# Longer DMA times in a planner, wider chunk spacing, split key buffers and one constant tile for two scans

## Chip, cores and metric

One NeuronCore of a Trainium2 chip runs the whole program in one launch. The metric is the device time of one execution in microseconds, and several executions are given by their median. The engines are named as in the profile: PE is TensorE, DVE is VectorE, ACT is ScalarE, POOL is GpSimd, and SP is the queue engine that issues nearly all DMAs of this kernel.

## What is computed

The reference has three stages, all in float32: a gated linear attention over 4 batches, 8 heads, 768 steps and 48 features, then two feed-forward stages over the 3072 tokens that come out of it.

```python
for t in range(S):                       # attention, S = 768
    state = alpha[:, :, t, :, None] * state + einsum('bhd,bhe->bhde', k[:, :, t], v[:, :, t])
    y[:, :, t] = einsum('bhd,bhde->bhe', q[:, :, t], state)
x = y.transpose(0, 2, 1, 3).reshape(3072, 384)
x = ((x @ w_a) * (x @ w_b)) @ w_out      # first feed-forward stage, 384 -> 1536 -> 384
h = x @ w_in                             # second, 384 -> 2048 -> 384
out = (maximum(h, 0) + alpha * minimum(h, 0)) @ w_out2
```

## The kernel before

**Tiling.** The tokens are cut into 6 blocks of 512 columns (`MB`). A block is made of four chunks of 128 steps, one for each batch, so there are 24 chunks, g = 4n + c for block n and batch c. The feed-forward matmuls run on pairs: each float32 operand is split into a high and a low part, and one product costs three passes (lines 926, 927 and 929). A *step* of the first stage is two up projections (tiles `pa` and `pb`, nine matmuls of 128x512 each) and, two steps later, the down projection (`acc`, nine matmuls); there are 12 steps a block. Blocks 0 and 1 are interleaved in halves, and blocks 2 to 5 follow whole. The second stage comes after all of the first, on results kept in DRAM.

**A chunk.** Its inputs come by three loads: `ra` (the decays, line 561), `kq` (keys and queries, line 565) and `v` (line 569). DVE runs a scan backwards (`scan_r`, line 584), a reciprocal of four columns (`recip`, line 590), a scan forwards (`scan_a`, line 594), and the product of both with keys and queries (`mul`, line 599). The first scan has a constant tile `ones` as its additive operand (zeros, and a one at the head of each of the four rows), the second a tile `invs` of the same form whose heads are the reciprocals. PE then computes scores, and two bursts follow: `pe_cross` (lines 786 and 808) and `pe_own` (lines 786 and 793, and from block 2 on also the scores of the next chunk, line 625). The last burst therefore waits for the next chunk's `mul` as well. Between the two bursts DVE updates the state (line 813, `As`).

From block 2 on (`BY_BLOCKS`) the keys are needed turned. DVE transposes them in 32x32 squares (`turn`, line 660), four DMAs store them in DRAM (`away`, line 664, `ktd<-kt`), and four bring them back (`back`, line 674, `ks<-ktd`). The tiles `kt` and `ks` share one buffer: line 678 lets the turn wait, through the ring `kring`, for the burst that used the keys of the chunk before.

**Buffers.** `ra`, `kq` and `v` have two buffers each. A `Ring` (line 281) hands over the operations that the next user of a buffer waits for. A `kq` load waits for all users of the chunk two earlier, its `pe_own` among them. The x tile of block n takes the buffer of block n-2 (line 1071).

**The order.** It is no written list. Each operation is handed to a planner, `Graph`, by `add` (line 81), with its engine, a planned duration, a key, and for a DMA a latency on top. `place` (line 112) lays the operations out in planned time: each engine takes the ready one with the lowest key. `latest` (line 199) goes back from the end and gives each its latest start as a new key. `search` (line 231) then moves keys of operations that begin before `SOON` = 120 us at random, 1500 times, and keeps what ends sooner on PE, also with durations and latencies drawn a little larger (`SEED`, `TRIES`, `WORLDS`, line 55). The program is emitted in the order found, and each engine executes its part strictly in that order. Where the plan has a pause of PE of over 0.5 us before the start of block 2, dummy matmuls are put in for 70% of it (`fill`, line 339, tile `wp`; they read `ones` without its first column).

**Keys and planned times that the change touches.** A chunk of block n from 2 on gets the key `block_at[n] - (BC - c) * 12000 - 14000` (line 535, in nanoseconds; `block_at` is the planned start of the block). Planned for its DMAs are, as duration plus latency in ns: `ra` 720 + 3000, `kq` 1400 + 3000, `v` 720 + 3000 (lines 577 to 579), each store of turned keys 430 + 2000 (line 680), each return 350 + 3800 (line 684). Between engines 250 ns (`HOP`) are added.

Of the kernel before, what the change touches and what calls it, by code (L numbers as in the profile page):

```python
# [14 lines left out]
F32 = mybir.dt.float32  # L15
BF16 = mybir.dt.bfloat16
# [4 lines left out]
ALU = mybir.AluOpType  # L21
# [4 lines left out]
P = 128  # L26
CH = 128
HC = CH // 2
BC = 4
MB = BC * CH  # L30
SQ = 32
BT = P // SQ
# [5 lines left out]
LAG = 2  # L38
SPLIT = ((0, 0), (1, 0))
BY_BLOCKS = 2  # L40

ON_PE = (("a", 0), ("b", 0), ("o", 0))

# [8 lines left out]
SLACK = 500  # L52
SWITCH = 100
SOON = 120000
SEED, TRIES, WORLDS = 2, 1500, 2


class Op:
# [10 lines left out]
class Graph:  # L69
# [11 lines left out]
    def add(self, eng, dur, fn, key, deps=(), lat=0, after=(), pool=None, burst=False, line=None):  # L81
        o = Op()
        o.pool, o.hold, o.burst = pool, [], burst
        o.eng, o.dur, o.fn, o.key, o.lat = eng, dur - LEAD.get(eng, 0), fn, key, lat + LEAD.get(eng, 0)
        o.users, o.soft, o.n = [], [], len(self.ops)
        for d in {x.n: x for x in deps if x is not None}.values():
            d.users.append(o)
        for d in {x.n: x for x in after if x is not None}.values():
            d.soft.append(o)
        if line:  # L90
            if line in self.last and self.last[line] not in [x for x in after if x is not None]:
                self.last[line].soft.append(o)
            self.last[line] = o
        self.ops.append(o)
        return o
# [203 lines left out]
def body(tc, akq, v, vg, w_a, w_b, w_o1, w_in, w_o2, beta, out):  # L299
    nc = tc.nc  # L300
# [5 lines left out]
    NJ = H // 2  # L306
    D = KT * P // H
    GR = 64 - D
    NA = NJ * (CH + 1) + 1
    NC = NJ * CH  # L310
    NB = NG // BC

    with ExitStack() as ctx:
        ctx.enter_context(tc.manual_schedule())
        pool = lambda name, bufs=1, **k: ctx.enter_context(tc.tile_pool(name=name, bufs=bufs, **k))
        const, wpool, pers = pool("const"), pool("wpool"), pool("pers")
        xpool, cpool, gpool, tp = pool("xpool", 2), pool("cpool", 2), pool("gpool", 2), pool("tp", 2)
# [7 lines left out]
        ident = plus.bitcast(F32)  # L325
        mask = const.tile([P, P], F32, name="mask")
        betaT = const.tile([P, F2], F32, name="betaT")
        ones = pers.tile([P, NJ, CH + 1], F32, name="ones")
        invs = pers.tile([P, NJ, CH + 1], F32, name="invs")
        Z = pers.tile([P, BC, NJ, D], F32, name="Z")  # L330
        At = pers.tile([P, 2 * NC], F32, name="As")
        x2d = [dram.tile([P, 2, KT, MB], F32, name=f"x2d{n}") for n in range(NB)]
        w2d = [dram.tile([P, 2 * UC], F32, name=f"w2d{i}") for i in range(2 * NU2)]
        ktd = [dram.tile([SQ, NJ, BT, P], F32, name=f"ktd{g}") for g in range(NG)]


        warm = ones.bitcast(BF16)[:, 0, 2 : 2 + 2 * CH]

        def fill(t0, t1):
            wp = ps_mm.tile([P, MB // 2], F32, name="wp", tag="mm")  # L340
            for _ in range(int((t1 - t0) * 0.7) // 110):
                nc.tensor.matmul(wp, warm[:, 0:P], warm, start=True, stop=True)

        nc.gpsimd.memset(ones, 0.0)
        nc.gpsimd.memset(ones[:, :, 0:1], 1.0)
        nc.gpsimd.memset(invs, 0.0)
        make_identity(nc, eye)
        nc.gpsimd.memset(mask, 1.0)
        nc.gpsimd.affine_select(
            out=mask, in_=mask, pattern=[[1, P]], compare_op=ALU.is_ge, fill=0.0,  # L350
# [18 lines left out]
        due, block_at = {}, {}  # L369
# [131 lines left out]
        for u in range(NU1):  # L501
            for nm, src in (("a", w_a), ("b", w_b), ("o", w_o1)):
                x = nm, u
# [16 lines left out]
        st = [dict() for _ in range(NG)]  # L520
        xt, xuse, xdone, xpart = {}, {}, {n: [] for n in range(NB)}, {}
        xring, lring, rring, vring = Ring(2), Ring(2), Ring(2), Ring(2)
        aring, kring, sring = Ring(1), Ring(1), Ring(1)
        both = ps_att.tile([P, 2, 2 * NC // 2], F32, name="both")
        yfree, afree = [], []
        att = lambda nm: ps_att.tile([P, NJ, CH], F32, name=nm, tag="att")
        before = {"scan": None}
        accfree = [[] for _ in range(KT)]
        state = [[] for _ in range(BC)]
        sums = [At[:, NC + i * NJ * D : NC + (i + 1) * NJ * D].rearrange("p (j d) -> p j d", d=D) for i in range(2)]  # L530
        slots = [Z[:, c] for c in range(BC)] + sums[1:]

        def place(g):
            n, c = divmod(g, BC)
            key = c * 1000 - 100000 if n == 0 else block_at[n] - (BC - c) * 12000 - 14000
            if n == 1:
                key = block_at[n] - (BC - c) * 9500 - 6000

            def A(eng, dur, fn, deps, early=0, lat=0, after=(), line=None):
                return G.add(eng, dur, fn, key - early, deps, lat, after, burst=eng == "PE", line=line)  # L540

            return st[g], n, c, n == 0, A

        def inputs(g):
            s, n, c, start, A = place(g)
# [28 lines left out]
            kT = lambda: s["kq"][:, 0]  # L574
            qT = lambda: s["kq"][:, 1]
            r0 = lambda: s["ra"][:, 0 : NA - 1].rearrange("p (j t) -> p j t", j=NJ)[:, :, 0:1]
            la = A("SP", 1000 if g == 0 else 720, load_a, rwait, 14000, 2400 if g == 0 else 3000, line="ra")
# [5 lines left out]
            def scan_r():  # L583
                nc.vector.tensor_tensor_scan(
                    out=s["ra"][:, 0 : NA - 1][:, ::-1], data0=s["ra"][:, : NA - 1 : -1],
                    data1=ones.rearrange("p j t -> p (j t)"), initial=0.0, op0=ALU.mult, op1=ALU.add,
                )

            def recip():
                nc.vector.reciprocal(invs[:, :, 0:1], r0())  # L590

            def scan_a():
                a = s["ra"][:, NA - 1 : 2 * NA - 2]
                nc.vector.tensor_tensor_scan(out=a, data0=a, data1=invs.rearrange("p j t -> p (j t)"),
                                             initial=0.0, op0=ALU.mult, op1=ALU.add)

            def mul():
# [1 line left out]
                nc.vector.tensor_tensor(out=s["kq"], in0=s["kq"], in1=f[:, :, :, 1:], op=ALU.mult)  # L599

            turned = n >= BY_BLOCKS
            r = A("DVE", 1220, scan_r, [la])
            rc = A("DVE", 180, recip, [r, before["scan"]])
            sa = before["scan"] = A("DVE", 1220, scan_a, [rc])
            slack = SLACK if not start else 0
            k1 = q1 = A("DVE", 1220, mul, [lq, sa], 0, slack)
            rhold.append(k1)
# [33 lines left out]
        def chunk(g):  # L641
            s, n, c, start, A = place(g)
# [3 lines left out]
            kT, qT, r0, r, k1, lv = (s[x] for x in ("kT", "qT", "r0", "r", "k1", "lv"))  # L646
# [9 lines left out]
                slots[c], slots[BC] = new, old  # L656

            def turn():
                s["kt"] = tp.tile([P, NJ, P], F32, name="kt", tag="ks", bufs=1)
                nc.vector.transpose(s["kt"], kT())  # L660

            def away(b):
                def f():
                    nc.sync.dma_start(
                        ktd[g].rearrange("t j a f -> t (j a) f")[:, :, b * SQ : (b + 1) * SQ],
                        s["kt"][b * SQ : (b + 1) * SQ].rearrange("p j (a d) -> p (j a) d", d=SQ),
                    )
                return f

            def back(a):  # L670
                def f():
                    if a == 0:
                        s["ks"] = tp.tile([P, NJ, P], F32, name="ks", tag="ks", bufs=1)
                    nc.sync.dma_start(s["ks"][a * SQ : (a + 1) * SQ], ktd[g][:, :, a, :])
                return f

            if turned:
                x = A("DVE", 650, turn, [k1, *kring.take()])
                lhold.append(x)
                moved = [A("SP", 430, away(b), [x], 0, 2000) for b in range(BT)]  # L680
                x = None
                back_at = []
                for a in range(BT):
                    x = A("SP", 350, back(a), moved, 0, 3800, after=[x])
                    back_at.append(x)

            zs = None
# [16 lines left out]
            if start:  # L704
# [3 lines left out]
                x = A("PE", 560, s["keys"], [k1, *w0])  # L708
                pa = A("PE", 1120, s["scores"], [k1, *w1, *w2])
            elif "front" in s:  # L710
                x = pa = s["front"]
# [5 lines left out]
            if turned:  # L717
                ks = back_at
# [531 lines left out]
```

## Time and profile before

| | us |
|---|---|
| median of 3 runs | 942.45 |
| lowest and highest | 941.32, 942.47 |
| the profiled execution | 943.25 |
| its span, first to last instruction | 941.50 |

| engine | busy us | share |
|---|---|---|
| PE | 932.5 | 99% |
| PE weight load | 760.1 | 81% |
| DVE | 564.0 | 60% |
| ACT | 245.2 | 26% |
| POOL | 2.2 | 0% |

The profile is of one execution, and its times count from the first instruction. Busy time doesn't tell useful from dummy matmuls; these have the tile `wp`. In the rows below a timeline gives start, duration, engine, line, operation and tiles (written <- read), and in brackets how long the engine had been idle before and who released it. "kq<-in_akq" is a load, "SPq" the issuing of DMAs on SP. The granted clock of PE is full in all stretches.

### The profile page before, as it was taken

The page shows a single profiled execution, that of the slowest core. Times are in us where ns is not written, and L with a number is a line of the kernel's source. Part 1 is how long each engine was busy: PE and PEld are TensorE (multiplying, and loading weights), DVE is VectorE, ACT ScalarE, POOL GpSimd, SP SyncE. Part 2 cuts the span into 40 slices and gives each one's busy share as a digit, 9 for nine tenths or more (in the row PEclk, how much of TensorE's full clock was granted, in tenths as well). Part 3 has the DMA queues.
Part 4 walks back from the last instruction along what each step waited for, and adds up shares of the span by engine and source line. Part 5 has one row for each costly group of instructions (what it writes and reads, how often), then busy time and mean ns, then how long its engine had stood idle before and what let it go on. Part 6 is the DMA issues. An engine that isn't in the chain of part 4 may idle for free.

```text
span 941.5 us, 15646 instructions
## 1 busy us (share of the span) xinstructions
PE 932.5 (99%) x6637; PEld 760.1 (81%) x6637; DVE 564.0 (60%) x865; ACT 245.2 (26%) x406; POOL 2.2 (0%) x11
## 2 busy tenths in 40 slices
PE   9999999999999999999999999999999999999998
PEld 7788887888888788787888888888888888888886
DVE  8999964674886687663232264554545545545554
ACT  3555531223333333331122121111111111111111
POOL 0000000000000000000000000000000000000000
PEclk9999999999999999999999999999999999999999
DMA  9973103563657767763266620100200200200000
GB/s 353 403 262 102 32 1 79 159 189 137 210 162 228 249 207 217 241 175 93 82 235 202 212 91 1 68 34 1 89 12 1 101 1 0 101 1 1 34 0 34
DMA packets 75238, 112.89 MB, mean 120 GB/s; under 512 B 38689, under 2 KB 48417, under 8 KB 75169
## 3 DMA queue, kind: packets, MB, share of 16 engines
q1 hardware_dynamic: 75024, 111.77, 36.1%
q8 instruction: 52, 0.85, 0.4%
q14 instruction: 18, 0.14, 0.0%
q10 hardware_dynamic: 144, 0.13, 0.0%
HBM read 78.97 MB, written 30.93 MB: 117 GB/s over the span
## 4 chain that ended last, share of the span: by engine, by line
PE 90%; DVE 5%; DMA 2%; issue 1%; SPq 1%; ACT 0%; DVEq 0%; ACTq 0%
PE acc L926 12%; PE acc L929 12%; PE acc L927 12%; PE pi L926 7%; PE pi L927 7%; PE pi L929 7%; PE pb L926 5%; PE pa L926 5%; PE pb L927 5%; PE pa L929 5%; PE pa L927 5%; PE pb L929 5%; PE both L786 2%; PE both L625 1%; DMA v<-in_v 1%; DMA ra<-in_akq 1%
## 5 line engine op out<-in xcount | busy, mean ns | idle before, releaser
L950 ACT CAST gh<-ng 128x512 fp32r<-128x512 f32 x96 | 59.5, 620 | 329.8 <-DVE ng L1163 274.0
L1159 DVE TENSOR_SCALAR ng<-pi,betaT 128x512 f32<-128x512 f32 x96 | 72.1, 751 | 105.6 <-PE pi L929 104.7
L954 DVE TENSOR_TENSOR gl<-ng,gh 128x512 fp32r<-128x512 f32 x96 | 66.3, 690 | 79.6 <-ACT gh L950 79.6
L926 PE MATMUL pi<-x,v 128*128 128x512 f32 x288 | 113.3, 393 | 0.0
L929 PE MATMUL acc<-gl,v 128*128 128x512 f32 x288 | 113.1, 393 | 0.0
L926 PE MATMUL acc<-gh,v 128*128 128x512 f32 x288 | 112.9, 392 | 0.0
L927 PE MATMUL pi<-x,v 128*128 128x512 f32 x288 | 112.7, 391 | 0.0
L927 PE MATMUL acc<-gh,v 128*128 128x512 f32 x288 | 112.1, 389 | 0.0
L1057 DVE TENSOR_TENSOR a_sb<-a_sb,pb 128x512 f32<-128x512 f32 (+1 forms) x76 | 49.9, 656 | 83.3 <-PE pb L929 83.3
L926 PE MATMUL pb<-x,wb 128*128 128x512 f32 (+1 forms) x228 | 87.8, 388 | 0.6 <-DVE a_sb L1057 0.6
L926 PE MATMUL acc<-gh,wo 128*128 128x512 f32 (+1 forms) x228 | 88.4, 388 | 0.0
L926 PE MATMUL pa<-x,wa 128*128 128x512 f32 (+1 forms) x228 | 87.3, 386 | 0.0
L929 PE MATMUL acc<-gl,wo 128*128 128x512 f32 (+1 forms) x228 | 86.8, 381 | 0.0
L927 PE MATMUL pb<-x,wb 128*128 128x512 f32 (+1 forms) x228 | 86.0, 380 | 0.5 <-DVE wb L453 0.5
L927 PE MATMUL acc<-gh,wo 128*128 128x512 f32 (+1 forms) x228 | 86.4, 379 | 0.0
L927 PE MATMUL pa<-x,wa 128*128 128x512 f32 (+1 forms) x228 | 85.9, 380 | 0.0
L950 ACT CAST gh<-a_sb 128x512 fp32r<-128x512 f32 (+1 forms) x76 | 45.3, 596 | 140.8 <-DVE a_sb L1057 131.5
L929 PE MATMUL pi<-x,v 128*128 128x512 f32 x288 | 81.6, 391 | 0.0
L1054 ACT COPY a_sb<-pa 128x512 f32<-128x512 f32 (+1 forms) x76 | 42.7, 562 | 107.1 <-PE pa L929 106.9
L1163 DVE SCALAR_TENSOR_TENSOR ng<-pi,ng 128x512 f32<-128x512 f32 x96 | 66.3, 691 | 3.1
L926 PEld LDWEIGHTS pi<-x,v 128*128 128x128 f32 x288 | 54.1, 188 | 13.7 <-DVE ng L1163 2.1
L954 DVE TENSOR_TENSOR gl<-a_sb,gh 128x512 fp32r<-128x512 f32 (+1 forms) x76 | 50.1, 659 | 25.0 <-ACT gh L950 24.9
(126 smaller groups left out, 1360.3 us busy)
## 6 DMA issues: line engine op xcount, KB each, us to landing
kq<-in_akq SPq DMA_DIRECT2D x24, 512.0 KB, 5.1
w2d<-ws SPq DMA_DIRECT2D x16, 768.0 KB, 5.1
v<-w2d SPq DMA_DIRECT2D x16, 768.0 KB, 5.9
x2d<-x SPq DMA_DIRECT2D x18, 512.0 KB, 3.7
x<-x2d SPq DMA_DIRECT2D x6, 1536.0 KB, 6.9
ra<-in_akq SPq DMA_DIRECT2D x24, 258.5 KB, 3.9
v<-in_v SPq DMA_DIRECT2D x24, 256.0 KB, 5.0
rs<-in_w_in SPq DMA_DIRECT2D x8, 768.0 KB, 6.0
```

Of the source, the lines that this page charges most:

```text
L625: nc.tensor.matmul(a[hs, i, j, :], kT()[ps, j, hs], qT()[ps, j, hs], start=True, stop=True, skip_group_check=True)
L786: nc.tensor.matmul(y_of(k, half(p), part_of(h)), s["v"][part_of(h), 2 * j + i, :], s["As"][part_of(h), i, j, :], start=first, stop=False, ...
L926: nc.tensor.matmul(o, lh, rh, start=first and n == 0, stop=False)
L927: nc.tensor.matmul(o, ll, rh, start=False, stop=False)
L929: nc.tensor.matmul(o, lh, rl, start=False, stop=last and n == len(pairs) - 1)
L950: nc.scalar.copy(gq[idx][0], src())
L954: nc.vector.tensor_tensor(out=gl, in0=src(), in1=gh.bitcast(F32), op=ALU.subtract)
L1054: nc.scalar.copy(b["a"], ba["t"])
L1057: nc.vector.tensor_tensor(out=b["a"], in0=b["a"], in1=bb["t"], op=ALU.mult)
L1159: nc.vector.tensor_scalar(out=b["n"], in0=bh["t"], scalar1=0.0, scalar2=betaT[:, i : i + 1], op0=ALU.min, op1=ALU.mult)
L1163: nc.vector.scalar_tensor_tensor(out=b["n"], in0=bh["t"], scalar=0.0, in1=b["n"], op0=ALU.max, op1=ALU.add)
```

## The change

- `add` gives every operation of SP with a key above `STEADY` = 110000 a planned latency longer by `SPARE` = 3500 ns.
- The chunks of blocks 2 to 5 get keys `PACE` = 16000 apart in place of 12000 (block 1 stays).
- The turned keys `kt` lie in an added part of the tile `As`, with a ring `tring` of their own: the turn waits for the stores of the chunk before. The loads of `ks` now wait for the burst that used `ks` before (`held`). Planned times: turn 700, stores 640 + 3500, returns 640 + 5000.
- `ones` and `invs` become one tile `heads`. The reciprocals overwrite its heads, and after the second scan POOL sets them back to one (`begin`, planned at 110 ns). The next chunk's first scan waits for that. One memset at the start is gone.
- The search has another seed, 6 in place of 2.

```diff
+PACE = 16000
+STEADY, SPARE = 110000, 3500
...
-SEED, TRIES, WORLDS = 2, 1500, 2
+SEED, TRIES, WORLDS = 6, 1500, 2
...
         o.pool, o.hold, o.burst = pool, [], burst
+        lat += SPARE if eng == "SP" and key > STEADY else 0
...
-        ones = pers.tile([P, NJ, CH + 1], F32, name="ones")
-        invs = pers.tile([P, NJ, CH + 1], F32, name="invs")
+        heads = pers.tile([P, NJ, CH + 1], F32, name="heads")
...
-        At = pers.tile([P, 2 * NC], F32, name="As")
+        At = pers.tile([P, NC + 2 * NJ * D + NC], F32, name="As")
...
-        warm = ones.bitcast(BF16)[:, 0, 2 : 2 + 2 * CH]
+        warm = heads.bitcast(BF16)[:, 0, 2 : 2 + 2 * CH]
...
-        aring, kring, sring = Ring(1), Ring(1), Ring(1)
+        aring, kring, sring, tring = Ring(1), Ring(1), Ring(1), Ring(1)
...
+        kt = At[:, NC + 2 * NJ * D :].rearrange("p (j t) -> p j t", j=NJ)
...
-            key = c * 1000 - 100000 if n == 0 else block_at[n] - (BC - c) * 12000 - 14000
+            key = c * 1000 - 100000 if n == 0 else block_at[n] - (BC - c) * PACE - 14000
...
+            def begin():
+                nc.gpsimd.memset(heads[:, :, 0:1], 1.0)
...
-            r = A("DVE", 1220, scan_r, [la])
-            rc = A("DVE", 180, recip, [r, before["scan"]])
-            sa = before["scan"] = A("DVE", 1220, scan_a, [rc])
+            r = A("DVE", 1220, scan_r, [la, before["scan"]])
+            rc = A("DVE", 180, recip, [r])
+            sa = A("DVE", 1220, scan_a, [rc])
+            before["scan"] = A("POOL", 110, begin, [sa])
...
-                x = A("DVE", 650, turn, [k1, *kring.take()])
+                x = A("DVE", 700, turn, [k1, *tring.take()])
                 lhold.append(x)
-                moved = [A("SP", 430, away(b), [x], 0, 2000) for b in range(BT)]
-                x = None
+                moved = [A("SP", 640, away(b), [x], 0, 3500) for b in range(BT)]
+                tring.use(*moved)
+                held, x = kring.take(), None
                 back_at = []
                 for a in range(BT):
-                    x = A("SP", 350, back(a), moved, 0, 3800, after=[x])
+                    x = A("SP", 640, back(a), [*moved, *held], 0, 5000, after=[x])
```

## Rows read from the trace of the kernel before

**Rows 1.** The page's first part: busy us, share of the span, instructions.
```profile
PE 932.5 (99%) x6637; PEld 760.1 (81%) x6637; DVE 564.0 (60%) x865; ACT 245.2 (26%) x406; POOL 2.2 (0%) x11
```
**Rows 2.** Sums by stretch: start:end length, busy us (instructions) of each engine, clock, DMA.
```profile
9.79:58.06 48.27, 47.09 (x672) 39.02 (x670) 47.77 (x87) 24.16 (x53) 0.00 (x0) 1.00 0.95 368
58.06:300.00 241.94, 241.94 (x2306) 197.87 (x2307) 180.91 (x289) 85.03 (x132) 0.00 (x0) 1.00 0.45 136
300.00:350.00 50.00, 49.87 (x570) 40.09 (x568) 37.56 (x62) 18.20 (x29) 0.00 (x0) 1.00 0.70 224
350.00:400.00 50.00, 49.34 (x362) 39.67 (x358) 37.27 (x58) 17.56 (x27) 0.00 (x0) 1.00 0.75 228
400.00:450.00 50.00, 47.97 (x556) 38.31 (x555) 23.73 (x37) 12.97 (x21) 0.00 (x0) 1.00 0.48 133
```
**Rows 3.** Timeline of PE, the two longest waits after 300 us.
```profile
430.25 0.46 PE L786 MATMUL both<-As,v 64*64 64x64 f32 x16 [2.03 <-DVE As L813]
...
384.59 0.50 PE L926 MATMUL pb<-x,wb 128*128 128x512 f32 x1 [0.64 <-DVE a_sb L1057]
```
**Rows 4.** Timeline of DVE before these two waits.
```profile
427.51 1.22 DVE L599 TENSOR_TENSOR kq<-kq,ra 128x1024 f32<-128x1024 f32 x1 [4.30 <-DMA kq<-in_akq]
429.88 0.32 DVE L813 TENSOR_TENSOR As<-both,Z 128x192 f32<-128x192 f32 x1
...
380.33 1.23 DVE L584 TENSOR_TENSOR_SCAN ra<-ra,ones 128x516 f32<-128x516 f32 x1 [4.15 <-DMA ra<-in_akq]
```
**Rows 5.** Timeline of the DMA issues on SP, 414.5 to 423 us.
```profile
414.98 3.35 SPq L664 DMA_DIRECT2D ktd<-kt  x4
420.00 2.50 SPq L674 DMA_DIRECT2D ks<-ktd  x4
422.54 0.59 SPq L565 DMA_DIRECT2D kq<-in_akq  x1
```
**Rows 6.** Timeline of PE around blocks 0 and 2, and a chunk's end.
```profile
154.22 0.85 PE L929 MATMUL pb<-x,wb 128*128 128x512 f32 x3
205.99 0.39 PE L926 MATMUL pa<-x,wa 128*128 128x512 f32 x1
416.02 0.65 PE L625 MATMUL both<-kq 48*64 48x64 f32 x32
```
**Rows 7.** Whom DVE waited for: us in all, times, longest us.
```profile
DVE kq L599 <- DMA kq<-in_akq: 27.4, 10, 5.4
DVE kt L660 <- PE both L808: 0.8, 1, 0.8
```
**Rows 8.** Timeline of POOL, and of PE's first dummy matmul.
```profile
1.38 0.10 POOL L345 MEMSET ones<- 128x4 f32 x1
...
1.38 0.39 PE L342 MATMUL wp<-ones 128*128 128x256 bf16 x1 [1.38 <-POOL ones L344]
```
**Rows 9.** Timeline of DVE at the start, and one step of weight preparation.
```profile
5.05 1.21 DVE L584 TENSOR_TENSOR_SCAN ra<-ra,ones 128x516 f32<-128x516 f32 x1
6.17 1.21 DVE L594 TENSOR_TENSOR_SCAN ra<-ra,invs 128x516 f32<-128x516 f32 x1
...
7.51 1.20 DVE L599 TENSOR_TENSOR kq<-kq,ra 128x1024 f32<-128x1024 f32 x1
...
40.54 0.56 DVE L434 TENSOR_SCALAR ra<-ra 128x768 uint32<-128x768 uint32 x1
```
**Rows 10.** Timelines of DVE and ACT: a cast between two steps of DVE.
```profile
375.48 0.69 DVE L954 TENSOR_TENSOR gl<-a_sb,gh 128x512 fp32r<-128x512 f32 x1 [0.69 <-ACT gh L950]
...
374.83 0.62 ACT L950 CAST gh<-a_sb 128x512 fp32r<-128x512 f32 x1 [2.56 <-DVE a_sb L1057]
```
**Rows 11.** Sums by stretch of the dummy matmuls alone: length, PE busy (instructions).
```profile
0.00:9.79 9.79, 8.41 (x57) 1.00 0.81 281
9.79:58.06 48.27, 3.25 (x24) 1.00 0.95 368
```
**Rows 12.** Sums by stretch of line 584 alone: length, DVE busy (instructions).
```profile
0.00:58.00 58.00, 9.67 (x8) 1.00 0.92 353
```

More of the change, by code (lines that the diff above doesn't have):

```diff
@@ L342, in fill @@
                 nc.tensor.matmul(wp, warm[:, 0:P], warm, start=True, stop=True)
-        nc.gpsimd.memset(ones, 0.0)
-        nc.gpsimd.memset(ones[:, :, 0:1], 1.0)
-        nc.gpsimd.memset(invs, 0.0)
+        nc.gpsimd.memset(heads, 0.0)
+        nc.gpsimd.memset(heads[:, :, 0:1], 1.0)
         make_identity(nc, eye)
@@ L585, in scan_r @@
                     out=s["ra"][:, 0 : NA - 1][:, ::-1], data0=s["ra"][:, : NA - 1 : -1],
-                    data1=ones.rearrange("p j t -> p (j t)"), initial=0.0, op0=ALU.mult, op1=ALU.add,
+                    data1=heads.rearrange("p j t -> p (j t)"), initial=0.0, op0=ALU.mult, op1=ALU.add,
                 )
             def recip():
-                nc.vector.reciprocal(invs[:, :, 0:1], r0())
+                nc.vector.reciprocal(heads[:, :, 0:1], r0())
+            def begin():
+                nc.gpsimd.memset(heads[:, :, 0:1], 1.0)
             def scan_a():
                 a = s["ra"][:, NA - 1 : 2 * NA - 2]
-                nc.vector.tensor_tensor_scan(out=a, data0=a, data1=invs.rearrange("p j t -> p (j t)"),
+                nc.vector.tensor_tensor_scan(out=a, data0=a, data1=heads.rearrange("p j t -> p (j t)"),
                                              initial=0.0, op0=ALU.mult, op1=ALU.add)
@@ L658, in turn @@
             def turn():
-                s["kt"] = tp.tile([P, NJ, P], F32, name="kt", tag="ks", bufs=1)
-                nc.vector.transpose(s["kt"], kT())
+                nc.vector.transpose(kt, kT())
             def away(b):
@@ L665, in f @@
                         ktd[g].rearrange("t j a f -> t (j a) f")[:, :, b * SQ : (b + 1) * SQ],
-                        s["kt"][b * SQ : (b + 1) * SQ].rearrange("p j (a d) -> p (j a) d", d=SQ),
+                        kt[b * SQ : (b + 1) * SQ].rearrange("p j (a d) -> p (j a) d", d=SQ),
                     )
```

## The prediction

> **What bounds the kernel now.** I read the busy table first, then the sums by stretch, then who TensorE (PE) waits for, then the timelines around those waits. PE is busy 932.5 us, 99% of the span [rows 1], so only what it waits, or what it does for nothing, can be saved. The stretches say where [rows 2]. Up to 9.79 us PE has nothing but dummy matmuls [rows 11]. From there to 58.06 us it is busy 47.09 of 48.27 us, and VectorE (DVE) 47.77: the start is paced by DVE. From 58.06 to 300 us PE lacks nothing. From 300 to 450 us it lacks 0.13 + 0.66 + 2.03 = 2.82 us, and nothing more while it still has chunks to do. The second half is a solid stream; no part of the change can shorten it.
>
> Each late wait has one story. At 428.2 us PE stops for 2.03 us until DVE's `As` update (line 813) is done [rows 3]. DVE had stood 4.30 us in front of the product on `kq` (line 599), because the load of that `kq` was still out [rows 4], and the update came behind it in DVE's order. SyncE (SP) had issued that load at 422.54, behind four `ktd` stores that took it from 414.98 to 418.33 and four `ks` loads from 420.00 to 422.50 [rows 5]. The chunk that had the buffer before gave it up with its last PE instructions, which end at 416.67 [rows 6], so the queue in front of the load cost nearly 6 us. The plan had booked the stores at 430 ns each and the loads at 350; four took 3.35 and 2.50 us. The 0.64 us wait at 383.95 is the same thing [rows 3, 4]: DVE stands 4.15 us before a scan for `ra`, and the MLP product `a_sb` queues behind it. The `kq` load itself took 427.51 - 422.54 = 5.0 us; the plan has 1.4 + 3.0 = 4.4.
>
> **Part by part.** *Longer DMAs in the plan, `PACE`.* No instruction is added. The plan gives each later SP operation 3.5 us more, so a `kq` load counts 7.9 us, and the key round trip is booked at 640 ns an issue. SP's order then puts the `kq` load ahead of the return of the keys, and DVE's order puts other work ahead of the product. The load that was 5 us under way, with 6 us of queue before it, now has 7.9 us in the plan after the PE instructions that free its buffer; 5.0 fits, so the three waits go: -2.82 us. What is late next? DVE waited ten times for `kq`, 27.4 us in all [rows 7], and nearly all of it was covered, since DVE is busy 24 to 38 of 50 us there [rows 2]. I therefore count the whole 2.82; the other end is 1.4, if a longer transfer or a different order returns half of it.
>
> Does the slower plan still fit? By the code, from the end of one chunk's last PE piece (which frees `kq`) to the first piece of the chunk two later it books 0.25 + 7.9 + 0.25 + 1.22 + 0.76 + 0.25 + 9.56 + 11.1 + 0.31 = 31.6 us, where before it was 16.3. Block 2 is the tightest place: its second chunk can't begin before block 0's last up projection is done with the x buffer, which ends near 154.9, and block 2's own first matmul stands at 205.99 [rows 6]. 157 for the second chunk's first piece, 5 to the end of its last, 31.6 by the plan, 5 for the last chunk: 199, so 7 us to spare. Other blocks have more. So no pause: 0.
>
> *Keys turned into their own space.* DVE's turn no longer waits for the piece that uses the keys before; the loads on SP now do, and behind them stand SP's next `kq`, `ra`, `v` and weight transfers. DVE waited for this just once, 0.8 us, hidden from PE [rows 7]. Gain 0; loss 0 as long as the `kq` load is ahead of them, else it is what is in the 1.4 above.
>
> *One constant tile.* Removed: one memset of POOL at the start, beside the first load: 0. Added: 24 memsets of 128x4; such a one took 0.10 us [rows 8]. New is the wait: the first scan of a chunk may start only when the second scan of the chunk before is done and the memset after it too. Behind that scan wait all of DVE's instructions, and PE, as long as DVE paces it, up to 58 us. At the very start it forbids the present order: the first scan of chunk 1 (5.05) fills the time before the second of chunk 0 (6.17) [rows 9]. Without it the second scan ends near 5.05 + 1.21 = 6.26, and the product on `kq`, which ran at 7.51 with its data there, may have to wait: between 0 (SP fetches `kq` before the second `ra`, which isn't wanted so early any more) and 7.51 - 6.26 = 1.25 us. Later hand-overs have a 1.2 us product to cover them; where one is bare it costs 0.10 plus two signals, and the path DVE to ScalarE to DVE shows 0.69 idle for a cast of 0.62, so 0.07 for both [rows 10]: 0.17 us. I take +0.4 for the whole start, nearer the cheap end because the planner knows these costs and orders round them.
>
> *Does the tile's double use bind PE?* The dummy matmuls read the same tile. They don't wait for writes to its first column: PE's first one starts at 1.38, when the memset of that column, 1.38 to 1.48, has just begun [rows 8]. 0.
>
> *A new search of the start.* With another seed and another graph the order of the first 120 us is drawn anew. Between 9.79 and 58.06 PE has 48.27 - 47.09 = 1.18 us of idle time and 3.25 us of dummy matmuls [rows 2, 11], so 4.43 us can be won at most; a worse draw can lose as much. No row favours a side: 0.
>
> **Sum.** The profiled execution took 943.25 us, a span of 941.5 and 1.75 around it. 943.25 - 2.82 + 0.4 = 940.83. It was 0.80 above the median of the three runs, 942.45, so I expect 940.0. About 0.2%, 1.9 us, is what a measurement of this kernel can tell from no change: the line is at 940.6.
>
> **The rivals.** *A better start* (0.12): waits gone and half of the 4.43 us won: 940.0 - 2.2 = 937.8. For it: dummy work is left there; against: DVE is busy 47.77 of 48.27 us.
>
> *Part comes back* (0.18): a late `kq` or `ks` transfer still holds DVE's queue, now at another chunk, since the `ks` loads wait on SP for the previous chunk: 940.0 + 1.4 = 941.4.
>
> *The change doesn't act* (0.04): the order around the last chunks stays, the 2.82 us too, and the start pays 0.4: 942.9.
>
> *Slower through the hand-over of the constant tile* (0.16). Place: the DVE-paced start, where eight first scans stand before 58 us [rows 12], so seven hand-overs. Price: if POOL's memset can't run while DVE is in one of its short integer steps, the weight preparation that stands between the scans (0.55 us each [rows 9]), a hand-over costs 0.55 + 0.17 = 0.72 us, seven of them 5.0, and the time is 942.45 - 2.82 + 5.0 = 944.6. It decides from 1.89 + 2.82 = 4.7 us on, 0.67 for each. For it: DVE has no spare time there; against: a product or mask of 0.6 to 1.2 us fits between, and before shows POOL and DVE at work at no common moment, so neither side is seen. The Trainium skill, "SBUF — State Buffer", section "Who interferes with whom", has a rule for this: a two-port VectorE step such as tensor_scalar and a GpSimd instruction lock one another out for the whole instruction, while one with two SBUF inputs, a scan or a product, only contends with GpSimd reads, which a memset doesn't make. By it the time would be up to the 944.6 of this rival, if each hand-over met such a step, and 940.0 if it met products; no run here shows it yet.
>
> **How the numbers follow.** The forecast has 0.50: 940.0, by itself 939.0 to 941.2, four fifths of it below 940.6. Faster: 0.40 + 0.12 = 0.52. Same: 0.10 + 0.18 + 0.04 = 0.32. Slower: 0.16. The range reaches from the better start, 937.8, to the slower rival, 944.6, where it leaves out the upper half of that case and a few hundredths below.
>
> **What the profile after would show.** Right: PE busy full from 300 to 450 us, DVE's idle time before line 599 small or covered, SP issuing `kq` before the four `ks` loads, and 9.8 to 58 us with some 4.4 us of dummies and waits as before. The slower rival: DVE idle before the first scan, released by POOL, several times 0.5 us before 58 us. Wrong altogether: dummy matmuls after 60 us (a planned pause, filled) or PE waits for `ks` or `kq` between 100 and 450 us.

## The result, and the profile after

The changed kernel takes 955.45 us (median of 4, 955.14 to 955.64), beside 942.46 for the kernel before on the same chip: the ratio is 1.0137 [1.0119, 1.0154], so it is slower by 1.4%. The forecast was 940.0, a gain of 0.25%, with a range up to 944.6; it was wrong, in size and in sign. The profiled execution took 955.37 us, its span is 953.7.

The page's first part of after, with the columns of [rows 1]:

```profile
PE 947.2 (99%) x6634; PEld 758.9 (80%) x6634; DVE 565.2 (59%) x865; ACT 245.9 (26%) x406; POOL 4.6 (0%) x34
```

PE ran three instructions fewer and was busy 14.7 us longer. It did not wait longer; its instructions took longer. The sums by stretch of after, columns as in [rows 2], say where:

```profile
9.79:58.06 48.27, 46.87 (x666) 38.42 (x665) 47.28 (x85) 24.41 (x53) 0.63 (x6) 1.00 0.96 364
58.06:300.00 241.94, 241.94 (x2341) 194.93 (x2340) 178.05 (x286) 83.18 (x132) 1.59 (x12) 1.00 0.46 134
300.00:350.00 50.00, 50.00 (x450) 39.88 (x449) 34.68 (x55) 16.34 (x25) 0.21 (x2) 1.00 0.65 197
350.00:400.00 50.00, 50.00 (x508) 39.80 (x507) 34.10 (x54) 16.48 (x26) 0.32 (x3) 1.00 0.67 204
400.00:450.00 50.00, 50.00 (x419) 39.82 (x418) 30.27 (x46) 15.55 (x25) 0.00 (x0) 1.00 0.57 176
...
600.00:700.00 100.00, 100.00 (x429) 79.83 (x428) 51.16 (x74) 16.67 (x28) 0.00 (x0) 1.00 0.13 48
```

From 300 to 450 us PE is busy in full: the 2.82 us of waits [rows 2, 3] are gone, as forecast. Its waits in all of after (engine, line, for whom: us in all, times, longest) are the first dummy matmul's and three of at most 0.7 us:

```profile
PE wp L344 <- POOL heads L346: 1.4, 1, 1.4
PE kps L637 <- PE dS L764: 0.7, 1, 0.7
PE kps L637 <- DVE kq L604: 0.3, 1, 0.3
PE both L779 <- DVE As L734: 0.3, 1, 0.3
```

The loss is in the last row of the sums. Between 600 and 700 us, in the second stage, PE has nothing but matmuls of 128x512 and never waits, at full clock, and gets through 429 of them. The kernel before does 436 in the same stretch, beside the same DMA traffic:

```profile
600.00:700.00 100.00, 100.00 (x436) 81.47 (x435) 51.87 (x74) 16.82 (x28) 0.00 (x0) 1.00 0.13 48
```

The timeline of PE (start, duration, line, tiles) shows it for single matmuls. Before, line numbers of the page:

```profile
600.64 0.39 PE L926 MATMUL acc<-gh,v 128*128 128x512 f32 x1
...
601.78 0.39 PE L929 MATMUL acc<-gl,v 128*128 128x512 f32 x1
```

After, six lines further down in the code:

```profile
99.75 0.28 PE L932 MATMUL acc<-gh,wo 128*128 128x256 f32 x1
...
100.69 0.28 PE L935 MATMUL acc<-gl,wo 128*128 128x256 f32 x1
...
599.68 0.40 PE L933 MATMUL acc<-gh,v 128*128 128x512 f32 x1
...
601.32 0.39 PE L933 MATMUL pi<-x,v 128*128 128x512 f32 x1
```

Before, five starts lie between 600.64 and 601.78, so 0.228 us each; after, seven between 599.68 and 601.32, 0.234 each. Over the whole trace the mean from one start to the next (gaps of over 300 ns left out, here and below) is 229.0 ns before and 233.3 after, in both stages alike. The program has 3564 matmuls of 128x512 (288 on each of six forms, 204 on each of nine): 3564 x 4.3 ns = 15.3 us. Matmuls of 128x256 kept their pace: eight starts lie between 99.75 and 100.69 in the rows above, 0.118 us each, and the mean is 117.6 ns in both traces (gaps of over 140 ns left out). The weight loads did not get longer either: 81.47 us for 435 of them before and 79.83 for 428 after, 187 ns each. So the question for the experiments is what slowed the 128x512 matmuls by 2% everywhere, also in a stage that the change doesn't touch.

### The profile page after: what moved, and what is told of

The parts are those of the page before. It is cut to its first block, busy times and chain, and to the rows that moved or that the text cites. A ratio compares the mean times of both kernels' runs of the same rounds, so it can differ in the third digit from the quotient of the medians.

```text
span 953.7 us, 15662 instructions
## 1 busy us (share of the span) xinstructions
PE 947.2 (99%) x6634; PEld 758.9 (80%) x6634; DVE 565.2 (59%) x865; ACT 245.9 (26%) x406; POOL 4.6 (0%) x34
## 4 chain that ended last, share of the span: by engine, by line
PE 96%; DVE 3%; issue 0%; ACT 0%; POOL 0%; ACTq 0%; POOLq 0%
PE acc L932 13%; PE acc L933 12%; PE acc L935 12%; PE pi L932 7%; PE pi L935 7%; PE pi L933 7%; PE pa L932 5%; PE pb L932 5%; PE pa L935 5%; PE pb L935 5%; PE pb L933 5%; PE pa L933 5%; PE both L792 2%; PE wp L344 1%; PE both L631 1%; PE both L814 1%
## 5 line engine op out<-in xcount | busy, mean ns | idle before, releaser
L932 PE MATMUL pi<-x,v 128*128 128x512 f32 x288 | 114.7, 398 | 0.0
L933 PE MATMUL acc<-gh,v 128*128 128x512 f32 x288 | 113.9, 395 | 0.0
L932 PE MATMUL acc<-gh,v 128*128 128x512 f32 x288 | 113.7, 395 | 0.0
L933 PE MATMUL pi<-x,v 128*128 128x512 f32 x288 | 113.4, 394 | 0.0
L935 PE MATMUL pi<-x,v 128*128 128x512 f32 x288 | 82.8, 395 | 0.0
L932 PEld LDWEIGHTS pi<-x,v 128*128 128x128 f32 x288 | 54.0, 187 | 15.4 <-DVE ng L1169 2.3
L935 PEld LDWEIGHTS pi<-x,v 128*128 128x128 f32 x288 | 54.0, 187 | 13.3
```

The costliest lines, as they stand in the source:

```text
L932: nc.tensor.matmul(o, lh, rh, start=first and n == 0, stop=False)
L933: nc.tensor.matmul(o, ll, rh, start=False, stop=False)
L935: nc.tensor.matmul(o, lh, rl, start=False, stop=last and n == len(pairs) - 1)
```

## The experiments

**The theories.** The second stage has the same 1728 matmuls of 128x512 in both kernels, at the same clock; in the order, some groups of nine have traded places. What can differ besides is where their operands lie. `ones` and `invs` took 2080 bytes of a partition each; one of them is gone, and `As` grew by 1536. Every tile allocated after these, `x`, `gh` and `gl` among them, lies 544 bytes lower; the weights don't move. In the compiled programs a weight tile starts at byte 51904 in both kernels, and `x` at 136960 before and 136416 after. Theory A: the moving operand (x, gh, gl) must start at a multiple of 64 bytes; 136960 does, 136416 doesn't. Its rival, theory B, was that the place doesn't matter and the new order or the new traffic does; theory C, that some other distance or the smaller total of the tiles does. When A fell (below), theory D took its place: what counts is the distance from the stationary operand (the weights) to the moving one, modulo 256 bytes. It was (136960 - 51904) mod 256 = 64 before and 32 after.

Unless another kernel is named, a diff is against the kernel after. "Spacing", and a figure in ns beside a time, is the mean from one 128x512 start to the next. Runs were made on several chips; each ratio is to the kernel before on the same chip.

**e1: the change with the old place.** 32 bytes behind `As` bring x to a multiple of 256 again, distance 64.

```diff
-        At = pers.tile([P, NC + 2 * NJ * D + NC], F32, name="As")
+        At = pers.tile([P, NC + 2 * NJ * D + NC + 8], F32, name="As")
-        kt = At[:, NC + 2 * NJ * D :].rearrange("p (j t) -> p j t", j=NJ)
+        kt = At[:, NC + 2 * NJ * D : 2 * NC + 2 * NJ * D].rearrange("p (j t) -> p j t", j=NJ)
```

> The changed kernel with 32 unused bytes a partition behind the tile As, so that all tiles allocated later (x, gh, gl, kq and so on) start 32 bytes higher, at a multiple of 64 as in the kernel before. Order, plan and instructions are the same. Theory A, the start address: every 128x512 matmul of the changed kernel takes 233.3 ns from start to start where it took 229.0, in all stretches alike, because its moving operand starts 32 bytes off a multiple of 64. Then the spacing falls back to 229.0, 3563 matmuls give back 3563 x 4.3 = 15.3 us, and the time is 955.4 - 15.3 = 940.1. Theory B, the new order or the new traffic (POOL's memsets, other DMA times) slows PE: nothing moves, 955.4. Theory C, the smaller total of the tiles: a distance between operands other than this counts, and 32 bytes change little of 955.4.

Measured: 940.06 us beside 942.22, ratio 0.9975 [0.9963, 0.9986]; spacing 229.0 ns. The sums by stretch of e1:

```profile
9.79:58.06 48.27, 46.91 (x665) 38.54 (x662) 47.83 (x86) 24.78 (x53) 0.64 (x6) 1.00 0.97 368
...
300.00:450.00 150.00, 150.00 (x1454) 121.22 (x1453) 99.62 (x156) 49.30 (x76) 0.53 (x5) 1.00 0.60 186
...
600.00:700.00 100.00, 100.00 (x437) 81.44 (x436) 52.19 (x75) 16.84 (x28) 0.00 (x0) 1.00 0.12 46
```

Thirty-two unused bytes, and nothing else, take 15.4 us out of the span (953.7 to 938.3). The order of all matmuls is that of after, so theory B falls, and theory C as it was put. That settles that the loss is the place of tiles, and that all else the change does comes to a small gain.

**e2: the old kernel, moved.** The other direction: 32 bytes behind `As` in the kernel before, with no other edit.

```diff
-        At = pers.tile([P, 2 * NC], F32, name="As")
+        At = pers.tile([P, 2 * NC + 8], F32, name="As")
```

> The kernel before with 32 unused bytes behind the tile As, nothing else: x, gh, gl and all later tiles start at 32 off a multiple of 64. Theory A: spacing 233.3 ns for the 128x512 matmuls, 942.5 + 15.3 = 957.8 us, with the order of before and its late waits of 2.8 us perhaps smaller, since PE is slower. Theory B: 942.5, nothing changes, as order and traffic are those of before. Theory C: 942.5, or a small part of the loss.

Measured: 956.11, ratio 1.014 [1.0117, 1.0164], 233.4 ns. The kernel before loses the same with none of the change in it (its distance is now 96, not 32).

**e3, e4, e7: other places.** As e1, with 16, 24 and 40 floats in place of 8 (64, 96 and 160 bytes; distances 96, 128 and 192).

```diff
+        At = pers.tile([P, NC + 2 * NJ * D + NC + 16], F32, name="As")   # e3; 24 in e4, 40 in e7
```

> The changed kernel with 64 unused bytes in place of 32: the later tiles move further, but again start at 32 off a multiple of 64. Theory A: no gain, 955.4 us and 233.3 ns. Theory C, distance or size: as good as the run with 32 bytes or better. Theory B: 955.4.

> The changed kernel with 96 unused bytes: the later tiles start at a multiple of 64, but not of 128 (x at 136512 = 1066 x 128 + 64), where the run with 32 bytes has multiples of 256. Theory A with a grain of 64 bytes: as the run with 32, 940.1 us and 229.0 ns. With a grain of 128 or 256 bytes: 955.4 or in between. Theory B: 955.4.

> The changed kernel with 160 unused bytes: x at 136576 = 1067 x 128, an odd multiple of 128. With 96 bytes (an odd multiple of 64) the spacing was 232.5 ns, with 32 (an even multiple of 128) 229.0. A grain of 128 bytes: 940.1 us, 229.0 ns. A grain of 256 or more: between 232.5 and 229.0, so 943 to 953 us. Theory D, a relation to the weights' place (192 beyond a multiple of 256): another value again, and the run with moved weights settles it.

Measured: e3 955.96, 1.0137 [1.0115, 1.0159]; e4 953.07, 1.0105 [1.0079, 1.0131], 232.7 ns; e7 954.11, 1.0117 [1.0087, 1.0147], 233.3 ns. In e4 and e7 x starts at a multiple of 64 bytes and is slow all the same: theory A falls. e1's place is special for another reason.

**e5: only x at the bad place.** A tile of 32 bytes goes ahead of gh and gl, which puts them at distance 64 while x stays at 32.

```diff
+        cpool.tile([P, 8], F32, name="gap", tag="gap", bufs=1)
```

> The changed kernel with an unused tile of 32 bytes between the buffers of x and those of gh and gl. So the moving operand of the up projections (x) stays at 32 off a multiple of 64, and that of the down projections (gh, gl) lies at a multiple of 256. Theory A, the start of the moving operand: pa, pb and pi stay at 233.3 ns, acc falls to 229.0; there are 1454 acc matmuls of 128x512 next to some 2050 of the others, so about 1500 x 4.3 = 6.4 us come back: 949. Theory D, one placement of the tiles decides for all matmuls: either 955.4 or 940.1.

Measured: 948.35, 1.0057 [1.004, 1.0074]. The matmuls that read x (`pa`, `pb`, `pi`) take 233 ns, the ones that read gh and gl (`acc`) 229. There are 204 x 6 + 288 x 3 = 2088 of the first kind (and 1476 of the second, not 1454); 2088 x 4.3 ns = 9.0 us, and 940.06 + 9.0 = 949.0. So it is each matmul's own operand that counts, not one of the kernel's other tiles.

**e6: only the weights moved.** The tile `betaT` lies ahead of the weights; 32 bytes more move them, and x moves with them by the same 32, back to a multiple of 256, with weights at 224 mod 256: distance 32.

```diff
-        betaT = const.tile([P, F2], F32, name="betaT")
+        betaT = const.tile([P, F2 + 8], F32, name="betaT")[:, 0:F2]
```

> The changed kernel with 32 unused bytes ahead of the weights: the weights (stationary operand) move to 32 off a multiple of 64, and x, gh and gl behind them to a multiple of 256. Theory A, only the moving operand counts: 940.1 us and 229.0 ns. Theory D, the distance between the weights and the moving operand counts (here it is that of the changed kernel, unchanged): 955.4 us and 233.3 ns. If the stationary operand's own start counts too, something in between or above.

Measured: 954.58, 1.0121 [1.0096, 1.0146], 233.3 ns. x lies as in e1, and the time is that of after. Of the moving operand alone no rule is left; both operands count, and theory D fits: same distance as after, same pace.

**e9, e10, e11: same distance, other places.** e9 takes the edits of e1 and e6 together (weights 224, x 32 mod 256). e10 moves the weights by 64 bytes and `As` by 32 (weights 0, x 64). e11 has 288 bytes behind `As` (weights 192, x 0, and a distance of 320 instead of 64 modulo 512). All three have distance 64 modulo 256.

```diff
+        betaT = const.tile([P, F2 + 8], F32, name="betaT")[:, 0:F2]      # e9; + 16 in e10
+        At = pers.tile([P, NC + 2 * NJ * D + NC + 8], F32, name="As")    # e9, e10; + 72 in e11
```

> The changed kernel with 32 unused bytes ahead of the weights and 32 behind As: weights at 224 beyond a multiple of 512, x, gh and gl at 288. Both are off every multiple of 64, but the moving operand lies 64 beyond the stationary one (modulo 256), as in the kernel before and in the run with 32 bytes behind As alone. Theory D, the distance between the two operands decides: 940.1 us, 229.0 ns. Theory A, the operands' own starts count (both have to be aligned): 955 us, 233 ns.

> The changed kernel with 64 unused bytes ahead of the weights and 32 behind As: weights at a multiple of 256, x, gh and gl 64 beyond one, where the run with 96 bytes had x at the same place and was slow (weights at 192, distance 128). Theory D: distance 64, so 940.1 us and 229.0 ns. Theory A (moving operand at a multiple of 256): as slow as the run with 96 bytes, 953.

> The changed kernel with 288 unused bytes behind As: x at a multiple of 512, weights at 192, a distance of 64 modulo 256 but of 320 modulo 512. Theory D with a period of 256 bytes: 940.1 us. With a period of 512 or more: another value, up to 956. Theory A: 940.1.

Measured: 940.45, 940.33 and 939.91, ratios 0.9978 [0.9967, 0.999], 0.9976 [0.9964, 0.9988] and 0.9968 [0.9956, 0.998], all at 229.0 ns. At this distance neither operand's own address matters, and 256 bytes is enough of a period.

**e12: distance zero.** Weights 0, x 0 modulo 256.

```diff
+        betaT = const.tile([P, F2 + 16], F32, name="betaT")[:, 0:F2]
+        At = pers.tile([P, NC + 2 * NJ * D + NC + 56], F32, name="As")
```

> The changed kernel with 64 unused bytes ahead of the weights and 224 behind As: weights and moving operands all at a multiple of 256, distance 0 modulo 256. Theory A (own starts): the best case, 940.1 us or below. Theory D: a distance not yet seen; it may be anything from below 229.0 to above 233.3 ns a matmul, and only distance 64 has been fast so far.

Measured: 934.26 (933.25 to 934.72) beside 942.27, ratio 0.9908 [0.9885, 0.993]; 227.2 ns. It is the fastest kernel here, and beats both. Sums by stretch of e12:

```profile
600.00:700.00 100.00, 99.99 (x440) 82.17 (x439) 52.57 (x76) 17.31 (x29) 0.00 (x0) 1.00 0.10 37
```

**e13: the same in the old kernel.** `ones` and `invs` come from the last pool, so that all between moves down by 4160 bytes, to distance 0.

```diff
-        ones = pers.tile([P, NJ, CH + 1], F32, name="ones")
-        invs = pers.tile([P, NJ, CH + 1], F32, name="invs")
+        ones = tp.tile([P, NJ, CH + 1], F32, name="ones", tag="ones", bufs=1)
+        invs = tp.tile([P, NJ, CH + 1], F32, name="invs", tag="invs", bufs=1)
```

> The kernel before with ones and invs in the pool that is laid out last, in place of the one between the weights and x; nothing else. Weights and x, gh, gl now all lie at 192 beyond a multiple of 256: distance 0, own starts off 256. Theory D, the distance decides, whatever the order: 227.1 ns a matmul as in the run at distance 0 of the changed kernel, 3563 x 1.9 = 6.8 us less, 935.5 us, and the late waits are as before or somewhat longer. Theory A (own starts): 942 or slower.

Measured: 937.68, ratio 0.9956 [0.9942, 0.997], 227.2 ns; 148.23 of 150 us busy from 300 to 450, so 1.77 us of its late waits are still there. The pace is the one that was expected, the time is not quite: the median lies 2.2 us above 935.5, with four runs from 936.47 (the profiled one) to 939.42. The gain by place doesn't need the change.

**e17, e18: the two distances left.** As e1 with 32 and 48 floats in place of 8: distances 160 and 224.

```diff
+        At = pers.tile([P, NC + 2 * NJ * D + NC + 32], F32, name="As")   # e17; + 48 in e18
```

> The changed kernel with 128 unused bytes behind As: x, gh and gl lie 160 beyond the weights modulo 256. Distances 32, 96, 128 and 192 took 232.5 to 233.4 ns a matmul, 64 took 229.0 and 0 took 227.1. If 64 is the one exception: 233 ns, 954 to 956 us. If odd multiples of 32 differ among each other: something else between 227 and 234 ns.

> The changed kernel with 192 unused bytes behind As: x, gh and gl lie 224 beyond the weights modulo 256, so 32 short of them. If nearness to distance 0 counted, 227 to 229 ns and 934 to 940 us; if the matmul's reads run ahead of the weights' by this place in a way that only 0 and 64 suit, 233 ns and 955 us.

Measured: 958.01, 1.0174 [1.0159, 1.0189], 234.3 ns, and 955.32, 1.0141 [1.0124, 1.0158], 233.3 ns. Sums by stretch of e17, the slowest place:

```profile
600.00:700.00 100.00, 100.00 (x427) 79.91 (x426) 50.56 (x73) 16.21 (x27) 0.00 (x0) 1.00 0.13 48
```

The map for 128x512, in steps of 32 bytes:

| distance mod 256 | ns from start to start | runs |
|---|---|---|
| 0 | 227.2 | e12, e13 |
| 32 | 233.3 | after, e6 (233 for x in e5) |
| 64 | 229.0 | before, e1, e9, e10, e11 (229 for gh, gl in e5) |
| 96 | 233.4 | e2, e3 |
| 128 | 232.7 | e4 |
| 160 | 234.3 | e17 |
| 192 | 233.3 | e7 |
| 224 | 233.3 | e18 |

The map doesn't hold for 128x256 matmuls. Nine of them in a row in e12 (distance 0), then in e7 (distance 192):

```profile
99.88 0.28 PE L932 MATMUL acc<-gh,wo 128*128 128x256 f32 x1
...
100.84 0.28 PE L935 MATMUL acc<-gl,wo 128*128 128x256 f32 x1
```
```profile
98.65 0.28 PE L932 MATMUL acc<-gh,wo 128*128 128x256 f32 x1
...
99.56 0.28 PE L935 MATMUL acc<-gl,wo 128*128 128x256 f32 x1
```

That is 0.96 / 8 = 0.120 us at the distance that is best for 128x512, and 0.91 / 8 = 0.114 at one that is bad for it; at 64 and at 32 it is 0.118. So this shape has a pace by distance too, in another order, and that it kept its pace between before and after is because 32 and 64 happen to be alike for it. The kernel has only 216 of them beside its dummies.

**e8: without the longer times and the wider spacing.** As e1, with these two parts undone. The new key buffers and their longer planned times stay.

```diff
-PACE = 16000
-STEADY, SPARE = 110000, 3500
+PACE = 12000
+STEADY, SPARE = 110000, 0
```

> The changed kernel with 32 unused bytes behind As (so its matmuls run at 229.0 ns), but PACE back at 12000 and SPARE at 0; the separate key buffers, their planned times, the constant tile and the seed stay. Theory of the prediction: the late waits are what the longer planned DMA times remove; without them PE waits 1 to 3 us between 300 and 450 us, and the time is 941 to 943. Rival: the planned times of the key round trip or the separate buffers alone remove them, and the time stays at 940.1.

Measured: 940.76, 0.9979 [0.9968, 0.999]. **e14: these two alone**, in the kernel before:

```diff
+PACE = 16000
+STEADY, SPARE = 110000, 3500
+        lat += SPARE if eng == "SP" and key > STEADY else 0
-            key = c * 1000 - 100000 if n == 0 else block_at[n] - (BC - c) * 12000 - 14000
+            key = c * 1000 - 100000 if n == 0 else block_at[n] - (BC - c) * PACE - 14000
```

> The kernel before with SPARE and PACE of the change alone (later DMAs planned 3.5 us longer, chunks from block 2 on 16000 apart); distance 64 as before. Theory of the prediction: this edit removes the 2.8 us of late waits: 939.5 us if the start comes out alike. Rival (from the run that has neither and has no late wait): the planned times of the key round trip do it, and here part of the waits stays, 941 to 942.5.

Measured: 942.38, 1.0007 [0.9998, 1.0015]. **e15: only the key trip's planned times**, in the kernel before:

```diff
-                x = A("DVE", 650, turn, [k1, *kring.take()])
+                x = A("DVE", 700, turn, [k1, *kring.take()])
-                moved = [A("SP", 430, away(b), [x], 0, 2000) for b in range(BT)]
+                moved = [A("SP", 640, away(b), [x], 0, 3500) for b in range(BT)]
-                    x = A("SP", 350, back(a), moved, 0, 3800, after=[x])
+                    x = A("SP", 640, back(a), moved, 0, 5000, after=[x])
```

> The kernel before with the planned times of the key round trip alone (turn 700, stores 640 + 3500, returns 640 + 5000 ns). Rival: the late waits go with it, 939.5 us if the start comes out alike. Theory of the prediction: a kq or ra load planned at 4.4 us still comes late, the waits stay in part, 941 to 942.5.

Measured: 942.23, 1.0001 [0.9992, 1.001]. The stretch 300 to 450 us in e8, e14 and e15, one fence each:

```profile
300.00:450.00 150.00, 150.00 (x1497) 121.03 (x1496) 99.15 (x154) 47.69 (x74) 1.52 (x5) 1.00 0.62 195
```
```profile
300.00:450.00 150.00, 150.00 (x1453) 121.20 (x1452) 102.27 (x158) 48.25 (x75) 0.00 (x0) 1.00 0.65 197
```
```profile
300.00:450.00 150.00, 148.47 (x1434) 118.73 (x1435) 97.10 (x151) 47.24 (x73) 0.00 (x0) 1.00 0.59 185
```

The late waits go with the longer times and wider spacing alone (e14), and also without them in e8, which has all the rest of the change: the key buffers, the longer planned trip, the constant tile and the new seed. The trip's times alone leave 1.53 us (e15); which of the other parts is needed in e8 was not tested. Yet e14 is no faster than before. Sums of its dummy matmuls alone, columns as in [rows 11]:

```profile
9.79:58.06 48.27, 2.04 (x16) 1.00 0.94 364
58.06:150.00 91.94, 0.00 (x0) 1.00 0.29 91
150.00:300.00 150.00, 3.34 (x29) 1.00 0.54 160
```

The 29 dummies stand from 209.6 to 212.9 us, right ahead of block 2. There the plan had a pause and filled it; the kernel before and e1 have no dummy after 58 us. 3.34 us come back for the 2.82 saved. (Its start is 1.5 us better: 2.04 of dummies and 0.93 idle from 9.79 to 58.06 us, where before has 3.25 and 1.18. The profiled span is only 0.5 us shorter, 941.0, the median no shorter.) Why the plan has the pause is open: e14 lacks not only the separate key buffers (with one buffer for `kt` and `ks` the turn of a key waits for the burst of the chunk before) but also the longer trip, the constant tile and seed 6. The buffers can't be the one condition: the planner alone, without a run on the chip, leaves the pause out of e14's plan when it gets these buffers, and just as well when it gets seed 6 and nothing else.

**e16: the old seed.** As e1.

```diff
-SEED, TRIES, WORLDS = 6, 1500, 2
+SEED, TRIES, WORLDS = 2, 1500, 2
```

> The changed kernel with 32 unused bytes behind As (distance 64) and the seed of before, 2 in place of 6. Theory of the prediction: the seed changes the start alone, where PE has 4.9 us of idle time and dummy matmuls between 9.8 and 58 us with seed 6; another draw moves the time by up to 2 us either way, 938 to 942, and the late waits stay away. Rival: seed 6 was what removed the late waits.

Measured: 941.15, 0.999 [0.9981, 0.9999]; 1.1 us above e1, which ran on another chip (the spans of the two profiles differ by 0.5 us). From 300 to 450 us PE is busy 150.00 of 150 us, so the seed isn't what removed the late waits. From 9.79 to 58.06 us it has 4.84 us of dummies and 1.18 idle, 1.1 more than e1. POOL's timeline in e16 (the bracket: idle before, released by), and DVE's at the second of the two memsets:

```profile
105.00 0.10 POOL L595 MEMSET heads<- 128x4 f32 x1 [10.29 <-DVE ra L599]
115.59 1.85 POOL L595 MEMSET heads<- 128x4 f32 x1 [10.49 <-DVE ra L599]
```
```profile
115.45 0.99 DVE L415 TENSOR_SCALAR c<-c 128x768 uint32<-128x768 uint32 x2
116.38 0.55 DVE L435 TENSOR_SCALAR ro<-ro 128x768 uint32<-128x768 uint32 x1
116.84 0.55 DVE L435 TENSOR_SCALAR ra<-ra 128x768 uint32<-128x768 uint32 x1
```

The memset that takes 0.10 us on its own takes 1.85 here, and ends at 117.44, as the last of four integer steps of DVE does (117.39). Beside a single such step (0.53 us) it takes 0.44, as at 44.06 and 78.34 us in e16.

## Why the prediction was wrong

**The step that failed.** "The second half is a solid stream; no part of the change can shorten it." I took from this that it can't lengthen it either, and the sum has a term for each instruction, wait and queue, but none for where tiles come to lie. Merging `ones` and `invs` and widening `As` were costed by what is executed: one memset less, 24 more. They also move every later tile by 1536 - 2080 = -544 bytes, which is -32 modulo 256, and take the matmul operands from distance 64 to distance 32. The missing term is 3564 x 4.3 ns = 15.3 us, and e1 measures it at 15.4 of span. None of the rivals held it: the slower one (944.6) was a wait, and the others were waits or dummies won or lost.

**Late waits, -2.82 us: right in size.** From 300 to 450 us PE is full in after and e1, and DVE's wait for `kq`, 27.4 us in ten waits before [rows 7], is 0.2 us in e1. The order on SP is the one forecast, the `kq` load ahead of the four `ks` loads, where [rows 5] had it behind. SP in e1:

```profile
405.50 2.60 SPq L669 DMA_DIRECT2D ktd<-As  x4
...
408.86 0.38 SPq L567 DMA_DIRECT2D kq<-in_akq  x1
409.30 2.44 SPq L571 DMA_DIRECT2D v<-in_v  x1
...
412.40 2.49 SPq L679 DMA_DIRECT2D ks<-ktd  x4
```

The load goes out 0.8 us after the last store's issue; in [rows 5] it went out 4.2 us after it. But my cause is not the only one that suffices: the waits are gone in e8 too, without the longer times and the wider spacing.

**"So no pause: 0", and "Keys turned into their own space: gain 0".** For the change as a whole there is no pause: no dummy stands after 58 us in after or e1. (Block 0's last up projection ends at 155.07 by [rows 6], not near 154.9, which changes nothing.) But "7 us to spare" says more than the runs bear out: e14, with the slower plan and the rest as before, has 3.34 us of dummies ahead of block 2, more than the late waits that it saves. What the key buffers are worth by themselves no run shows, since none has the change without them alone.

**The start, +0.4 us: not decided.** From 9.79 to 58.06 us after has 1.40 us idle and 3.52 of dummies, 0.49 more than before [rows 2, 11]; up to 9.79 its dummies are 8.34 us against 8.41. In all that is 0.42 us lost, the forecast to the digit. But e1, with the same order, has 1.36 + 3.53 us and only 7.68 up to 9.79: a gain of 0.27 over before. In e11, again the same order, 7.18 us stand there, a gain of 0.8. So single executions of one order differ at the start by over a microsecond, and no sign of so small a term can be read from them. The dummies of e1, columns as in [rows 11]:

```profile
0.00:9.79 9.79, 7.68 (x50) 1.00 0.77 276
9.79:58.06 48.27, 3.53 (x26) 1.00 0.97 368
```

The 1.25 us of bare waiting for `kq` didn't come: the product follows its scan without idle time in DVE's timeline of e1, as its load now goes out second (issued at 1.24, before at 1.71):

```profile
5.04 1.23 DVE L599 TENSOR_TENSOR_SCAN ra<-ra,heads 128x516 f32<-128x516 f32 x1
6.31 1.22 DVE L604 TENSOR_TENSOR kq<-kq,ra 128x1024 f32<-128x1024 f32 x1
```

**The search's draw, 0.** With the place mended, the two seeds differ by 1.1 us in their medians and 0.5 in their profiled spans (e16, e1), inside the bound of 4.43.

**The hand-over of the constant tile.** The rival's mechanism exists: in e16 a memset waits out DVE's integer steps, 1.85 us instead of 0.10. By the Trainium skill, "SBUF — State Buffer", section "Who interferes with whom", a VectorE step in a two-port mode, which tensor_scalar can be in, and a GpSimd instruction lock one another out; the row agrees. It cost nothing here: no DVE idle time is released by POOL in after, e1 or e16, since the next scan comes later than the memset's end. The rival was refuted in its place, the first 58 us, where the seven memsets of after take 0.10 or 0.11 us each.

**The sum with the place undone.** 941.50 - 2.82 - 0.27 = 938.41 for the span; e1 has 938.3. The 0.27 is e1's own, so this checks only the 2.82. That e1's median of 940.06 is 0.06 from the 940.0 forecast is in part luck: the same order took 940.45, 940.33 and 939.91 in e9 to e11, and the start's +0.4 is within what executions differ by. None of this rescues the forecast: the kernel that was asked about has the 15.3 us.

**The signs I named** were fulfilled in after: full PE from 300 to 450, `kq` early on SP, 1.40 + 3.52 = 4.92 us of waits and dummies at the start, no late dummies. They all looked at waits, and the loss was in busy time. The row that shows it is the first of the page: busy up by 14.7 us with three instructions fewer.

## What to carry to other kernels

A change of a tile's size moves every tile allocated after it, and in a kernel bound by matmuls that can cost more than the edit itself is worth: before costing it, work out how far the moving and the stationary operands move against each other, and keep their distance, or set it for the shape that most of the time goes to. When a result surprises, compare counts in a stretch without waits first: the same busy time with fewer instructions points at the instructions' own pace, not at the schedule. And undo the side effect alone (here 32 unused bytes) before judging the change.

## What was not expected of the hardware

The pace of a 128x512 float32 matmul, with its weight load beside it, depends on the distance between its two operands in SBUF: 227.2 ns at 0 modulo 256 bytes, 229.0 at 64, 232.7 to 234.3 at the six other multiples of 32, at a granted clock of 1.00 (2.4 GHz) throughout. Over this kernel that is 934.26 to 958.01 us. The Trainium skill, "TensorE: Matmul & The Clock Gate", section "Step-by-step: what each phase is for", gives about 216 ns from one matmul of 512 columns to the next, and "SBUF — State Buffer", "Who interferes with whom", has the moving operand and the weight load on independent ports with PE waiting for no one. Neither has a term for where the operands lie. The runs show one, up to 7.1 ns a matmul (227.2 to 234.3), and no run here comes down to 216; the measurement decides.

Open is what that is. That reads of weights and of moving data meet in the same part of a memory is argued from the period of 256 bytes, and not shown. Open too is why 128x256 matmuls order the distances otherwise (0.120 us at 0, 0.118 at 32 and 64, 0.114 at 192). All weights of this kernel lie alike modulo 256, so whether the distance that counts is to the weights in use or to those being loaded can't be told. Distances that are no multiple of 32 bytes, and other types (the profile's f32 is float32r in the program), were not tried.
